# Linear attention, a routed mixture of experts and a gated layer on one core: two routing batches of four tiles, and three last tiles by one-hot matmuls

## The chip, the cores and the metric

The kernel runs on one core of a Trainium2 chip. Its engines work beside each other and meet through semaphores: TensorE (PE in the profile; PEld is its weight load), VectorE (DVE), ScalarE (ACT), GpSimd (POOL) and SyncE (SP), which issues most DMAs. The metric is the device time of one execution in microseconds; a kernel is judged by the median of several executions.

## What is computed

Three layers follow each other; everything is float32.

```python
# linear attention with decay, B, H, S, D = 2, 8, 768, 48
for t in range(S):
    cur = einsum('bhd,bhe->bhde', u * k[t], v[t])
    y[t] = einsum('bhd,bhde->bhe', r[t], state + cur)
    state = w * state + einsum('bhd,bhe->bhde', k[t], v[t])
# top-1 mixture of 8 experts over N = 1536 tokens of 384 values
expert = argmax(x @ w_gate); gate = softmax(x @ w_gate)[expert]
# token i takes the next free place of its expert (dropped past the capacity)
out[i] = gate[i] * (relu(x[i] @ w1[expert]) @ w2[expert])
# gated layer
g = x @ moe2_w_gate
return (silu(g) * (x @ moe2_w_val)) @ moe2_w_out
```

## The kernel before

The 1536 tokens are 12 tiles of 128 (NT). `attention` is a pipeline over the iterations `it`, from -4 to 12, written out by hand: the order of the calls in its loop is the order of the instructions on each engine. In iteration `it` PE makes the outputs of tile `it` (`outputs`), the token-major form and logits of tile `it` (`token_major`, into PSUM tile xl), and the inner products of tile `it + 2` (`inner`, into A). DVE multiplies in the decays of tile `it + 3` (RK), sums its diagonal factor c, and copies the masked inner products (COPY_PREDICATED). ACT builds the diagonals AT from c, and copies the outputs out of PSUM (xT, line 324; xl waits for it) and the token-major rows (xu, line 520).

Routing runs beside this in batches of tiles, listed in BATCHES. A batch whose last tile is `it - 1` is routed in iteration `it`: `route1` on DVE (lines 531 to 538) ends in the one-hot `oh` of the chosen experts, `place_pe` counts places on PE (pos, line 551), `route2` on DVE (lines 558 to 583) turns pos into the gate value m and the row in the DRAM table x_disp. Then each tile of the batch is scaled by its gate value on ACT (`scale`, line 591) and scattered into x_disp by an indirect DMA of POOL (`issue`, line 597). Tiles wait in a list `to_scatter`: an iteration scales one at its start and scatters it later, and certain iterations take extra ones out of turn.

Expert 0 would have to wait for the last tiles to arrive in x_disp. So the last NLAST tiles go into its input also by matmul: route2 makes for each a 128 x 224 one-hot `hot` (line 577, with a second `rows` call, line 571, ahead of it), and `first_add` (line 349) multiplies the tile's rows by it, three matmuls, summed in PSUM. The earlier tiles come by a DMA: `x_load` reads expert 0's first 224 rows from x_disp into xr0 (SP, line 675), issued as soon as the last tile that is not in this group has been scattered; `first_rows` (line 357) adds them to the same sum. The tiles of the group are scattered too, since another expert may need them, and those scatters wait until xr0 has been read. The last LATE tiles are routed one by one at the front of their iterations. Before, the group is tiles 8 to 11. In iteration 12 PE runs first_add of tile 10, first_add of tile 8, pos of tile 11, first_rows and first_add of tile 11; then the experts begin (line 822).

Of the kernel before, what the change touches and what calls it, by code (L numbers as in the profile page):

```python
# [11 lines left out]
F32 = mybir.dt.float32  # L12
# [11 lines left out]
P = 128  # L24
B, H, S, D = 2, 8, 768, 48
NCH = S // P
NT = B * NCH
HP = H // 2
DM = H * D
# [24 lines left out]
UC = KD * 256  # L54


NLAST, LATE = 4, 3

BATCHES = [(0, 3), (3, 6), (6, 8), (8, 9), (9, 10), (10, 11), (11, 12)]
NBT = 3  # L60
FF_WEIGHTS = {"w_gate": [P, KD, 256], "w_val": [P, KD, 256], "w_out": [P, 2, DM]}

W_LO, W_HI = 0.6, 1.6
# [6 lines left out]
class Kernel:  # L70
# [47 lines left out]
    def attention(self, st):  # L118
        tc, nc, a = self.tc, self.nc, self.a
        tp = self.tp = self.pool(st, "tp")  # L120
# [116 lines left out]
        xTs = self.xTs = {}  # L237
        self.xl, self.xu, self.batches, self.to_scatter, self.scaled = {}, {}, BATCHES, [], []
        self.row = cp.tile([P, NT], I32, name="row")

        def decay(i):
            RK[i] = tp.tile([P, 2, HP, P], F32, name="RK", tag="RK", bufs=4)

            for h in (slice(0, 2), slice(2, HP)) if i == 0 else (slice(0, HP),):
                decays[i] = nc.vector.tensor_mul(RK[i][:, :, h], rkT[i % NB][:, :, h], W2[:, :, h])
# [18 lines left out]
        def diag_act(i):  # L264
            AT[i] = tp.tile([P, 2, HP, P], F32, name="AT", tag="AT", bufs=3)
            c = cc.pop(i)
            for j in range(2):
                for hp in range(HP):
                    nc.scalar.activation(AT[i][:, j, hp], ident, AF.Copy, scale=c[:, j, hp:hp + 1])  # L269
# [35 lines left out]
        def outputs(i):  # L305

            for hp in range(HP):
                for j in range(2):
                    rows = slice(64 * j, 64 * j + D)
                    z = self.zero[rows, 0:D] if i % NCH == 0 else Z[i % 2][rows, hp]  # L310
                    nc.tensor.matmul(
                        y[rows, hp], lhsT=z, rhs=RK[i][rows, 0, hp],
                        start=(hp == 0), stop=False, skip_group_check=True,
                    )
            for hp in range(HP):
                for j in range(2):
                    nc.tensor.matmul(
                        y[64 * j:64 * j + D, hp], lhsT=head(v_all, i, 2 * hp + j), rhs=AT[i][:, j, hp],
                        start=False, stop=True, skip_group_check=True,
                    )  # L320

        def d_major(i):
            xT = xTs[i] = tp.tile([P, HP, P], F32, name="xT", tag="xT", bufs=2)
            nc.scalar.copy(xT, y)
            del RK[i], AT[i]
# [18 lines left out]
        def first_add(i, first, last):  # L344
            xu, _, hot = self.last[i]
            if first:
                px.extend(self.pa_tile() for _ in range(KD))
            for k in range(KD):
                nc.tensor.matmul(
                    px[k][:, 0:BLK], lhsT=xu[:, k * P:(k + 1) * P], rhs=hot, start=first, stop=last,  # L350
                    skip_group_check=True,
                )

        def first_rows(first):
            for k in range(KD):
                for t in range(2):
                    nc.tensor.matmul(
                        px[k][:, t * BP:(t + 1) * BP], lhsT=self.xr0[:, t, k * P:(k + 1) * P],
                        rhs=ident[0:BP, 0:BP], start=first, stop=first, skip_group_check=True,
                    )  # L360

        ok = lambda i: 0 <= i < NT
        has_state = lambda i: ok(i) and i % NCH < NCH - 1
        ends = {hi - 1: (lo, hi) for lo, hi in BATCHES}

        def issue():

            i = self.scaled[0][0]
            self.issue()
            if i == NT - NLAST - 1:  # L370
                self.x_load(0, self.xr0)
# [8 lines left out]
        for it in range(-4, NT + 1):  # L380

            if self.to_scatter:
                self.scale()
                if it >= NT - 3:
                    issue()
            batch = ends.get(it - 1)
            late = it - 1 >= NT - LATE
            if ok(it - 1):
                self.logits(it - 1)
            if ok(it):  # L390
                outputs(it)
                if not late:
                    d_major(it)
            if it == 0:
                diag_act(2)
            if batch:
                self.route1(*batch)
            if late:
                if ok(it):
                    d_major(it)  # L400
                if it - 2 >= NT - LATE:
                    first_add(it - 2, it - 2 == NT - LATE, False)
                if it == NT:
                    for i in range(NT - NLAST, NT - LATE):
                        first_add(i, False, False)
                self.place_pe(*batch)
                self.route2(*batch)
                if it == NT:
                    first_rows(False)
                    first_add(NT - 1, False, True)  # L410
            if has_state(it + 1):
                state_update(it + 1)
            if ok(it + 3):
                decay(it + 3)
                load_T(it + 3 + NB)
            if it < 0 and ok(it + 2):
                inner(it + 2)
            if ok(it + 3):
                diag_dve(it + 3)

                if it != -1:
                    diag_act(it + 3)
            if it < 0 and ok(it + 4):
                diag_pool(it + 4)
            if has_state(it + 1) and (it + 1) % NCH:
                op = state_decay(it + 1)
                if ok(it + 3):
                    behind(op, decays[it + 3])
            if it >= 0 and ok(it + 4):
                behind(diag_pool(it + 4), decays[it + 3])  # L430
            if ok(it + 4):
                keys_pool(it + 4)
                load_rk(it + 4 + NB)
            if it >= 0 and ok(it + 2):
                inner(it + 2)
            if batch and not late:
                self.place_pe(*batch)
            if self.scaled:
                issue()

            if it == NT - 5 or it == NT - 3:
                self.scale()
                issue()
            if batch and not late:
                self.route2(*batch)
            if it == -1:
                self.route_inputs(wg, cap_i)
            if it in (-1, 2, 4):
                load_v({-1: 3, 2: 6, 4: 9}[it])
            if it in (-2, 0):  # L450
                first = (it + 2) // 2 * ST
                self.clear_rows(self.x_disp[first:first + BLK])
            if ok(it):
                self.token_major(it)
            if has_state(it + 2):
                state_pe(it + 2)
            self.prefetch(it)
            if it in WARMS:
                warm(WARMS[it])
# [11 lines left out]
    def psum_rooms(self, u=False):  # L471

        bank = self.ps_1.tile([P, 512], F32, name="bank")
        n = NBT * E
        self.lgs = [bank[:, i * n:(i + 1) * n].rearrange("p (t e) -> p t e", e=E) for i in range(2)]
        self.rev = bank[:, 2 * n:2 * n + E]
        self.rank = bank[:, 2 * n + E:2 * n + E + NBT]
        self.sum = bank[:, 2 * n + E + NBT:2 * n + E + 2 * NBT]
        return bank[:, 512 - DM:] if u else None

    def route_rooms(self):
# [4 lines left out]

        self.ex = tp.tile([P, NBT, E + 1], F32, name="ex")

# [25 lines left out]
    def logits(self, i):  # L514
        nc, tp, xl = self.nc, self.tp, self.xl.pop(i)
        t = i - max(lo for lo, _ in self.batches if lo <= i)
        self.lg = self.lgs[sum(lo <= i for lo, _ in self.batches) % 2]
        nc.vector.tensor_reduce(self.lg[:, t], xl[:, :, 2 * D:].rearrange("p h e -> p e h"), AX.X, ALU.add)
        xu = self.xu[i] = self.last[i][0] if i in self.last else tp.tile([P, DM], F32, name="xu", tag="xu", bufs=6)
        nc.scalar.copy(xu.rearrange("p (h d) -> p h d", h=HP), xl[:, :, 0:2 * D])  # L520

    def route1(self, lo, hi):
# [3 lines left out]
        over_tiles = lambda x: x.unsqueeze(1).to_broadcast([P, n, E])  # L526
        small = lambda name: tp.tile([P, NBT, E], F32, name=name, tag=name, bufs=1)[:, 0:n]
        lg, oh = self.lg[:, 0:n], self.oh[:, lo:hi]
        m = self.m = tp.tile([P, 5, NBT], F32, name="m", tag="m", bufs=4)[:, :, 0:n]
        dif, eqr = small("dif"), small("eqr")  # L530
# [702 lines left out]
```

## Time and profile before

| What | us |
|---|---|
| Median of 3 runs | 453.38 (453.3 to 454.85) |
| The profiled execution | 451.36 |
| Its span, from the first to the last instruction | 449.6 |
| PE busy in the span | 432.4 (96%) |
| DVE, ACT, POOL busy | 295.1, 212.4, 156.1 |
| First matmul of the experts starts at | 79.19 |

The page of the profile gives busy time of each engine; the busy table by stage cuts the span into stretches; a timeline lists the instructions in order of time, and in brackets how long the engine stood idle before one and what ended that. A row such as `59.32 0.92 PE L512` is an instruction of line 512 that started at 59.32 us and took 0.92 us, merged with its neighbours of the same kind where it ends with x6. A float32 matmul leaves two records, so three matmuls show as x6.

### The profile page before, as it was taken

What the parts mean: (1) busy time and instruction counts of PE and PEld (TensorE: products, weight loads), DVE (VectorE), ACT (ScalarE), POOL (GpSimd) and SP (SyncE); (2) the same over time, 40 slices, a digit from 0 to 9 for tenths busy, and PEclk for the clock granted to TensorE, in tenths of its full rate; (3) what the DMA queues carried; (4) which work ended last, traced back from release to release, by engine and by line L of the source; (5) the groups of instructions that cost most, each with busy time, mean ns of one, the idle gap of its engine ahead of it and who ended that gap; (6) DMA issues with size and microseconds to landing.
All of it is one profiled execution on the core that took longest, in us unless ns stands there. A gap on an engine that the chain in (4) does not pass through costs nothing. (4 is left out here: it accounts for less than half of the span.)

```text
span 449.6 us, 8438 instructions
## 1 busy us (share of the span) xinstructions
PE 432.4 (96%) x3211; PEld 418.3 (93%) x3211; DVE 295.1 (66%) x578; ACT 212.4 (47%) x469; POOL 156.1 (35%) x147
## 2 busy tenths in 40 slices
PE   7899999999999999999999999999999999999991
PEld 7788878989999999999998999999999999999991
DVE  7989986887877977986557888979865111111110
ACT  1687774636756756755555534343343031230310
POOL 5745652201121220000343555555546233332321
PEclk9899999999999999999999999999999999999996
DMA  7998942599999999602022423242300100001001
GB/s 255 315 357 281 398 165 85 161 362 261 330 219 266 203 293 275 231 1 72 1 70 71 137 85 125 77 140 81 131 2 0 53 1 19 36 0 54 2 20 40
DMA packets 24802, 63.78 MB, mean 142 GB/s; under 512 B 4784, under 2 KB 10032, under 8 KB 24752
## 3 DMA queue, kind: packets, MB, share of 16 engines
q1 hardware_dynamic: 22112, 57.43, 40.5%
q0 software_dynamic: 1920, 4.73, 2.9%
q10 hardware_dynamic: 720, 1.00, 0.8%
q8 instruction: 27, 0.44, 0.4%
q14 instruction: 23, 0.19, 0.1%
HBM read 55.67 MB, written 7.48 MB: 140 GB/s over the span
## 5 line engine op out<-in xcount | busy, mean ns | idle before, releaser
L1034 POOL TENSOR_TENSOR al<-sg,ah 128x384 fp32r<-128x384 f32 x48 | 54.1, 1128 | 132.9 <-ACT ah L1033 132.9
L667 DVE TENSOR_TENSOR wlo<-raw,whi 128x768 fp32r<-128x768 f32 x60 | 57.2, 954 | 9.4 <-ACT whi L666 8.5
L799 PE MATMUL py<-hc,whi 128*128 128x448 f32 x192 | 63.1, 370 | 0.0
L1033 ACT CAST ah<-sg 128x384 fp32r<-128x384 f32 x48 | 24.7, 514 | 78.0 <-DVE sg L1030 78.0
L810 PE MATMUL A<-xc,whi 128*128 128x224 f32 x336 | 57.7, 276 | 1.0 <-DVE xc L683 0.9
L800 PE MATMUL py<-hc,wlo 128*128 128x256 f32 x192 | 53.8, 280 | 0.0
L810 PEld LDWEIGHTS A<-xc,whi 128*128 128x128 f32 x336 | 51.2, 192 | 1.9 <-DVE xc L683 1.5
L666 ACT CAST whi<-raw 128x768 fp32r<-128x768 f32 x60 | 49.9, 838 | 0.7 <-PE py L799 0.7
L1047 PE MATMUL po<-w_out_hi,ah 128*128 128x384 f32 x144 | 48.6, 337 | 0.0
L1049 PE MATMUL po<-w_out_hi,al 128*128 128x384 f32 x144 | 48.5, 337 | 0.0
L1048 PE MATMUL po<-w_out_lo,ah 128*128 128x384 f32 x144 | 48.5, 337 | 0.0
L810 PE MATMUL A<-xc,wlo 128*128 128x224 f32 x168 | 46.2, 275 | 0.0
L877 POOL DMA_INDIRECT ids<-tok,by_expert x12 | 13.9, 1162 | 75.0 <-DMA ids<-tok,by_expert 66.6
L1056 DVE TENSOR_TENSOR acc<-acc,po 128x384 f32<-128x384 f32 x36 | 19.3, 546 | 30.9 <-PE po L1049 30.9
L799 PEld LDWEIGHTS py<-hc,whi 128*128 128x128 f32 x192 | 36.0, 188 | 2.6
L1030 DVE TENSOR_TENSOR sg<-A,sg 128x384 f32<-128x384 f32 x24 | 13.3, 555 | 37.0 <-PE A L1027 29.3
L800 PEld LDWEIGHTS py<-hc,wlo 128*128 128x128 f32 x192 | 36.5, 190 | 0.0
L1030 DVE TENSOR_TENSOR sg<-g,sg 128x384 f32<-128x384 f32 x24 | 13.3, 555 | 34.5 <-PE g L1027 27.6
L269 ACT ACTIVATE AT<-ident,c 128x128 f32<-128x128 f32 x96 | 29.3, 389 | 9.1 <-DVE c L260 9.0
L829 ACT ACTIVATE hc<-A 128x224 fp32r<-128x224 f32 x64 | 23.1, 362 | 21.3 <-PE A L810 18.6
L810 PEld LDWEIGHTS A<-xc,wlo 128*128 128x128 f32 x168 | 32.2, 192 | 0.0
L1029 ACT ACTIVATE sg<-A 128x384 f32<-128x384 f32 x24 | 11.6, 484 | 33.8 <-PE A L1027 33.8
(171 smaller groups left out, 1106.3 us busy)
## 6 DMA issues: line engine op xcount, KB each, us to landing
raw<-in_w SPq DMA_DIRECT2D x62, 384.0 KB, 6.8
rkT<-in_rkT SPq DMA_DIRECT2D x12, 512.0 KB, 5.4
rk<-in_rk SPq DMA_DIRECT2D x12, 384.0 KB, 6.4
raw<-in_w_gate SPq DMA_DIRECT2D x6, 768.0 KB, 4.2
raw<-in_w_val SPq DMA_DIRECT2D x6, 768.0 KB, 4.2
raw<-in_w_out SPq DMA_DIRECT2D x6, 768.0 KB, 4.3
x_disp<-zero SPq DMA_DIRECT2D x8, 336.0 KB, 7.1
xr<-x_disp SPq DMA_DIRECT2D x8, 336.0 KB, 6.1
```

What stands on the lines that cost most here:

```text
L269: nc.scalar.activation(AT[i][:, j, hp], ident, AF.Copy, scale=c[:, j, hp:hp + 1])
L666: nc.scalar.copy(h_, raw)
L667: nc.vector.tensor_sub(l_, raw, h_.bitcast(F32))
L799: nc.tensor.matmul(ps[:, 0:2 * BLK], lhsT=wh, rhs=xc, start=first, stop=False, skip_group_check=True)
L800: nc.tensor.matmul(ps[:, 0:256], lhsT=wl, rhs=xc[:, 0:256], start=False, stop=last, skip_group_check=True)
L810: self.nc.tensor.matmul(ph[:, HI], lhsT=w[:, k, fs], rhs=x[1][:, k, half], start=(k == 0 and i == 0), stop=(k == KD - 1 and i == 2),)
L1030: nc.vector.tensor_mul(sg, pg["w_val"], sg)
L1033: nc.scalar.copy(h_, sg)
L1034: nc.gpsimd.tensor_sub(l_, sg, h_.bitcast(F32))
L1047: nc.tensor.matmul(po, lhsT=ah[:, ts_], rhs=wh, start=(i == 0), stop=False)
L1048: nc.tensor.matmul(po, lhsT=ah[:, ts_], rhs=wl, start=False, stop=False)
L1049: nc.tensor.matmul(po, lhsT=al[:, ts_], rhs=wh, start=False, stop=(i == len(parts) - 1))
```

## The change

Two batches of four tiles take the place of (0, 3), (3, 6) and (6, 8); the pools that hold a batch grow from three tiles to four, and the tile pool xu from six buffers to eight. NLAST falls from 4 to 3, so tile 8 has no one-hot and no first_add, and x_load follows the scatter of tile 8 instead of that of tile 7. Iteration 9 (NT - 3) takes three tiles out of turn instead of one; iteration 7 (NT - 5) still takes one.

```diff
-NLAST, LATE = 4, 3
-
-BATCHES = [(0, 3), (3, 6), (6, 8), (8, 9), (9, 10), (10, 11), (11, 12)]
-NBT = 3
+NLAST, LATE = 3, 3
+
+BATCHES = [(0, 4), (4, 8), (8, 9), (9, 10), (10, 11), (11, 12)]
+NBT = 4
...
-            if it == NT - 5 or it == NT - 3:
+            for _ in range({NT - 5: 1, NT - 3: 3}.get(it, 0)):
                 self.scale()
                 issue()
...
-        xu = self.xu[i] = self.last[i][0] if i in self.last else tp.tile([P, DM], F32, name="xu", tag="xu", bufs=6)
+        xu = self.xu[i] = self.last[i][0] if i in self.last else tp.tile([P, DM], F32, name="xu", tag="xu", bufs=8)
```

On ACT in iterations 7 to 9 there stood before (xu written by L591 is a scaling in place, by L520 the copy of a tile's rows; xu_209 is tile 8's copy, xs_210 its scaled rows):

```order
L591 ACTIVATE xu<-xu,m 128x384 x2
L520 COPY xu<-xl 128x384
L324 COPY xT<-y 128x512
L533 ACTIVATE ex<-dif 128x2x8
L269 ACTIVATE AT<-ident,c 128x128 x8
L591 ACTIVATE xu<-xu,m 128x384
L520 COPY xu_209<-xl 128x384
L324 COPY xT<-y 128x512
L533 ACTIVATE ex<-dif 128x8
L591 ACTIVATE xu<-xu,m 128x384
L591 ACTIVATE xs_210<-xu_209,m 128x384
```

And now, from the same scaling of iteration 7:

```order
L591 ACTIVATE xu<-xu,m 128x384
L520 COPY xu<-xl 128x384
L324 COPY xT<-y 128x512
L533 ACTIVATE ex<-dif 128x4x8
L269 ACTIVATE AT<-ident,c 128x128 x8
L591 ACTIVATE xu<-xu,m 128x384
L520 COPY xu<-xl 128x384
L324 COPY xT<-y 128x512
L533 ACTIVATE ex<-dif 128x8
L591 ACTIVATE xu<-xu,m 128x384 x4
```

The pair ahead of xT of tile 8 (the first L324 of each list) has become one scaling; after the exp of tile 8, four scalings (tiles 5 to 8) stand where there were two (tiles 7 and 8).

On POOL, the scatters (L597) from iteration 7 on, before (L378 is the decay of the state, xs_210 to xs_219 are tiles 8 to 11):

```order
L597 DMA x_disp<-xu,row 14080x384 x2
L378 TENSOR_TENSOR Z_134<-zt,sq 112x192
L597 DMA x_disp<-xu,row 14080x384 x2
L378 TENSOR_TENSOR Z_135<-zt,sq 112x192
L597 DMA x_disp<-xu,row 14080x384
L597 DMA x_disp<-xs_210,row 14080x384
L597 DMA x_disp<-xs_213,row 14080x384
L597 DMA x_disp<-xs_216,row 14080x384
L597 DMA x_disp<-xs_219,row 14080x384
```

And now (xs_210 to xs_216 are tiles 9 to 11):

```order
L597 DMA x_disp<-xu,row 14080x384 x2
L378 TENSOR_TENSOR Z_134<-zt,sq 112x192
L597 DMA x_disp<-xu,row 14080x384
L378 TENSOR_TENSOR Z_135<-zt,sq 112x192
L597 DMA x_disp<-xu,row 14080x384 x4
L597 DMA x_disp<-xs_210,row 14080x384
L597 DMA x_disp<-xs_213,row 14080x384
L597 DMA x_disp<-xs_216,row 14080x384
```

Behind the last decay stand four scatters (tiles 5 to 8) ahead of the load of xr0, where one (tile 7) stood; tile 8's was behind the load.

On PE from xl of tile 11 to the count, before (hot_211 belongs to tile 8, hot_217 to tile 10, hot_220 to tile 11):

```order
L512 MATMUL xl<-IW,xT 128x104 x4
L349 MATMUL A<-hot_217,xu_215 128x224 x3
L349 MATMUL A<-hot_211,xu_209 128x224 x3
L551 LDWEIGHTS before
L551 MATMUL pos<-oh,before 128x8
L551 LDWEIGHTS ones_bf
L551 MATMUL pos<-ohs,ones_bf 128x8
L357 MATMUL A<-ident,xr 128x112 x6
L349 MATMUL A<-hot_220,xu_218 128x224 x3
```

And now (hot_214 belongs to tile 10, hot_217 to tile 11):

```order
L512 MATMUL xl<-IW,xT 128x104 x4
L349 MATMUL A<-hot_214,xu_212 128x224 x3
L551 LDWEIGHTS before
L551 MATMUL pos<-oh,before 128x8
L551 LDWEIGHTS ones_bf
L551 MATMUL pos<-ohs,ones_bf 128x8
L357 MATMUL A<-ident,xr 128x112 x6
L349 MATMUL A<-hot_217,xu_215 128x224 x3
```

The three matmuls of tile 8 between those of tile 10 and pos of tile 11 are gone.

## Rows read from the trace of the kernel before

**Rows 1.** Busy by stage: stretch, length, PE, PEld, DVE, ACT, POOL, clock, DMA share, GB/s.

```profile
36.00:60.00 24.00, 23.60 (x357) 20.26 (x356) 22.64 (x60) 19.94 (x59) 15.36 (x17) 1.00 0.89 329
79.20:97.00 17.80, 17.75 (x105) 17.11 (x103) 15.25 (x39) 8.72 (x17) 2.78 (x3) 1.00 0.74 239
```

**Rows 2.** Timeline, 57 to 60 us: start, duration, engine, line, operation [idle before].

```profile
57.32 1.11 ACT L591 ACTIVATE xu<-xu,m 128x384 f32<-128x384 f32 x2
...
58.20 1.33 POOL L597 DMA_INDIRECT x_disp<-xu,row  x1 [1.53 <-ACT xu L591]
...
58.69 0.58 ACT L324 COPY xT<-y 128x512 f32<-128x512 f32 x1
...
59.32 0.92 PE L512 MATMUL xl<-IW,xT 128*128 128x104 f32 x6 [0.37 <-ACT xT L324]
```

**Rows 3.** Timeline, 64 to 68.5 us (end of iteration 9, iteration 10).

```profile
64.17 1.34 DVE L283 COPY_PREDICATED AT<-mask,A 128x512 f32<-128x512 uint8 x2 [0.73 <-PE A L276]
64.68 1.01 POOL L597 DMA_INDIRECT x_disp<-xu,row  x1 [0.17 <-issue]
...
66.17 0.15 DVE L571 SCALAR_TENSOR_TENSOR m<-bank,placeall 128x1 f32<-128x1 f32 x1
66.35 0.62 ACT L591 ACTIVATE xs<-xu,m 128x384 f32<-128x384 f32 x1 [2.08 <-DVE m L571]
...
66.67 0.15 DVE L571 SCALAR_TENSOR_TENSOR row<-bank,placeall 128x1 int32<-128x1 f32 x1
...
66.94 0.19 DVE L518 TENSOR_REDUCE bank<-xl 128x8 f32<-128x32 f32 x1
...
67.16 0.48 ACT L520 COPY xu<-xl 128x384 f32<-128x384 f32 x1 [0.19 <-DVE bank L518]
...
67.43 0.33 SPq L675 DMA_DIRECT2D xr<-x_disp  x1
...
67.74 0.57 ACT L324 COPY xT<-y 128x512 f32<-128x512 f32 x1
...
68.18 0.17 PE L551 MATMUL pos<-oh,before 128*128 128x8 bf16 x1 [0.98 <-DVE oh L538]
...
68.36 0.36 PE L512 MATMUL xl<-IW,xT 128*128 128x104 f32 x1
```

**Rows 4.** Timeline of PE, 74 to 80 us (iteration 12).

```profile
74.08 2.54 PE L349 MATMUL A<-hot,xu 128*128 128x224 f32 x12 [0.23 <-DVE hot L577]
76.46 0.17 PE L551 MATMUL pos<-oh,before 128*128 128x8 bf16 x1
...
76.51 1.57 PE L357 MATMUL A<-ident,xr 112*128 112x112 f32 x12
77.95 1.37 PE L349 MATMUL A<-hot,xu 128*128 128x224 f32 x6
```

**Rows 5.** Timeline of DVE, 75 to 79.5 us (routing of tile 11).

```profile
75.25 0.16 DVE L538 TENSOR_TENSOR oh<-eqr,bank 128x8 bf16<-128x8 f32 x1
...
76.69 0.17 DVE L562 SCALAR_TENSOR_TENSOR sc<-pos,oh 128x8 f32<-128x8 f32 x1 [0.99 <-PE pos L551]
...
77.41 0.40 DVE L577 TENSOR_SCALAR hot<-slot,m 128x224 f32<-128x224 f32 x1
```

**Rows 6.** Timeline of POOL, 57 to 80 us: scatters of tiles 8 and 9.

```profile
71.23 0.96 POOL L597 DMA_INDIRECT x_disp<-xs,row  x1 [5.54 <-DVE bank L559]
72.49 0.96 POOL L597 DMA_INDIRECT x_disp<-xs,row  x1 [0.30 <-ACT xT L324]
```

**Rows 7.** DMA issues, 66 to 70 us, then the whole span: KB, us to landing.

```profile
xr<-x_disp SPq DMA_DIRECT2D x1, 336.0 KB, 3.0
xr<-x_disp SPq DMA_DIRECT2D x8, 336.0 KB, 6.1
```

**Rows 8.** Busy table by stage around the early fall of the granted clock.

```profile
14.40:15.80 1.40, 0.06 (x3) 0.09 (x5) 1.37 (x4) 0.43 (x2) 1.34 (x2) 1.00 0.92 309
15.80:19.30 3.50, 3.50 (x42) 3.01 (x44) 3.03 (x5) 2.02 (x7) 3.50 (x3) 0.51 0.87 300
```

## The prediction

> **What bounds the kernel now.** I read the busy table by stage first. From 79.2 us on, TensorE (PE) is busy almost without a break (17.75 of 17.80 us in the next stage), and nothing there is touched, so whatever moves the start of the first expert (the 79.2 us mark) moves the end by as much. From 36 to 60 us PE is busy 23.60 of 24.00 us while VectorE (DVE) has 22.64 [rows 1]: PE is the bound of the steady loop, and DVE work taken away there is worth only what PE waits for. So I looked next, on the timelines, for each place where PE waits in the iterations that change, and for what ends that wait. There are three.
>
> At 59.32 us PE waits 0.37 us for the ScalarE (ACT) copy xT of tile 8. That copy stands behind two scalings in a row (1.11 us from 57.32) and begins at 58.69 [rows 2]. At 68.18 PE waits 0.98 us for the one-hot `oh` of tile 9, made on DVE. DVE had started the copies of iteration 9 at 64.17 (after PE), then ran route2 of tile 8 until 66.94, then the logits and route1 of tile 9; behind it ACT makes scaling, xu and xT, and xT of tile 10 (67.74 + 0.57) releases xl at 68.36 [rows 3]. From 74.08 on PE runs 12 matmul records of first_add without a wait, six of tile 10 and six of tile 8, then pos, first_rows and first_add of tile 11 [rows 4].
>
> **The change part by part.** *Batches.* Seven batches become six. The batch that goes (tiles 3 to 5) is 12 small DVE instructions like those of [rows 3], 0.15 to 0.19 us each, about 2 us in iteration 6; but PE bounds that stage, so by itself this is worth nothing; of the small pos matmuls 18 become 17. What counts is where the scalings land: ACT no longer has two in a row ahead of xT of tile 8 (its list shows one, since the four tiles of the first batch are scaled over iterations 5 to 7 and the second batch is not routed yet). One scaling less is about half of 1.11 us, more than the 0.37 us that PE waits. **Term 1: 0.37 us.** Bounds: 0, if c, which DVE hands to ACT, comes later, and 0.55, half of the pair.
>
> *Tile 8 leaves the one-hot group (NLAST 4 to 3).* On DVE, route2 of tile 8 loses the second `rows` and `hot`: from 66.17 to 66.67, 0.50 us, between PE's inner of iteration 9 and the logits of tile 9 [rows 3]. So the logits of tile 9 come 0.37 + 0.50 = 0.87 us earlier, at 66.07, and `oh` lets PE go at 67.31. PE's own outputs move by 0.37 only, so the wait there falls to about 0.48 us. But xl of tile 10 wants xT, and ACT is next in line: the scaling of tile 8 starts after m, now 66.17 - 0.37 = 65.80, plus 0.03 and 0.62 is 66.45; its successor overlaps by some 0.05, so xu starts at 66.40 rather than 67.16, and xT and xl move by 0.76, not 0.87. **Terms 1 and 2 together: 0.76 us** at xl of tile 10 (68.36 to 67.60); bounds 0.39 (term 1 at nothing) and 1.05 (term 1 at 0.55, ACT not in the way).
>
> On PE the six records of first_add of tile 8 go. Twelve take 74.08 to 76.46, so six take 1.19 us [rows 4]. They were cover: `oh` of tile 11 is written at 75.25 to 75.41 [rows 5], and 0.76 us earlier is 74.65. PE is done with tile 10 at 74.08 - 0.76 + 1.19 = 74.51 and then waits for it until about 74.70. pos of tile 11 thus moves from 76.46 to 74.70. Behind it first_rows (76.51 to 77.95, 1.44 us) hides `hot` of tile 11: DVE took 1.12 us from sc at 76.69 to the end of hot at 77.81 [rows 5], so hot is ready at 74.93 + 1.12 = 76.05, and PE comes to first_add of tile 11 at 74.75 + 1.44 = 76.19. **Term 3: 1.00 us** (1.19 less 0.19 of uncovered wait); bounds 0.9 and 1.19.
>
> *The scatters and the load xr0.* This is what could spoil it. The load of expert 0's rows now follows tile 8's scatter instead of tile 7's, and the second batch's four scalings all fall into iteration 9. On ACT three scalings of about 0.55 us sit after exp of tile 8; before the change ACT stood idle 2.08 us ahead of tile 8's scaling [rows 3], which covers the two that are new there. On GpSimd (POOL) one scatter, a decay and four scatters now stand in a row. Before, the scatter behind the decay began at 64.68 [rows 3], now 0.37 earlier, 64.31. Three more steps of 1.18 us (1.01 + 0.17 of issue, the spacing of rows behind other work), or 1.26 us as 71.23 to 72.49 shows [rows 6], put tile 8's scatter at 67.85 to 68.09; I take 1.26, a real pair of scatters. Its scaling is done at 66.45, so POOL sets the time. SyncE (SP) began the load at 67.43 after a scatter begun at 64.68, 2.75 us; the load landed in 3.0 us [rows 3, 7]. That gives 68.09 + 2.75 + 3.0 = 73.84. first_rows wants it at 74.75, so 0.9 us of slack hides it. If each scatter took the longest seen, 1.33 us [rows 2], with 0.17 of issue, the load lands at 74.56, still in time. Scatters 9 to 11 must wait until this load has been read, as tile 8's did at 71.23 [rows 6]; tile 11's own scaling is later than that, so they delay nothing. Nothing but expert 1's load waits behind xr0 on SP, and that waits for the last scatter anyway. **Term 4: 0.**
>
> *Sizes.* The wider pool of xu and the wider batch tiles change addresses; the batch instructions grow from 24 to 32 columns on an engine with room in that stage [rows 1]: nothing.
>
> Sum: 0.76 + 1.00 = **1.76 us**. The profiled execution, 451.36 us with a span of 449.6, would become 449.6 with a span of 447.8. The median of the runs is 453.38, so it lies 2.0 us above the profiled one; I take the gain off the median: **451.6 us**, which is 0.39% less. A measurement of this kernel tells about 0.5%, 2.27 us, from no change, so the forecast lies inside "same", on the fast side. By the terms' bounds the gain is 1.3 to 2.2 us, 451.2 to 452.1.
>
> **The rivals.** *A little more (451.0 us).* Term 1 is 0.55, ACT does not hold xT of tile 10, `oh` of tile 11 is no wait: 1.05 + 1.19 is 2.24, and some 0.1 from smaller waits that DVE's lead removes in iterations 4 to 7. For it: DVE has two microseconds less to do. Against: PE had next to no idle time there to give back [rows 1].
>
> *The scatters stretch (452.4 us).* If the load lands about 0.8 us after first_rows wants it, half of the gain is gone. For it: five scatters now lie on one queue. Against: the scatter at 64.68 ran through a DVE copy (64.17, 1.34 us) and took 1.01 us [rows 3], no longer than others. The Trainium skill, SBUF — State Buffer, section "Who interferes with whom", says that descriptor generation on GpSimd is locked out while certain copies, casts and tensor_scalar instructions of VectorE hold the shared port. By that rule the copy beside a scatter would add its 1.34 us to the row, and the load would land at 75.2, some 0.4 us late; the scatter beside the copy here shows no such stretch, so I give it little.
>
> *Slower (455.5 us).* The load lands as late as the median of its eight kind, 6.1 us instead of 3.0 [rows 7]: 76.94 instead of 73.84. First_rows then starts 0.4 us later than before, and PE has stood idle for 2.2 us. That has a price of its own: after 1.40 us with 0.06 us of PE work the granted clock was 0.51 for 3.5 us, the 1.2 GHz level [rows 8], which costs 3.5 x 0.49 = 1.7 us. Together 2.1 us above the median. It decides from a landing of about 5.7 us. Against: the 6.1 belongs to loads beside the weight stream; here the weight loads are over and the one measured in this place took 3.0. The Trainium skill, TensorE: Matmul & The Clock Gate, section "HAM oscillation — how this bites in real kernels", says that gaps between matmuls caused by waiting for a load throttle the clock again; this trace agrees at 15.8 us, and shows no drop after the 0.98 us gap at 68.18.
>
> *It doesn't do what it says.* If xT of tile 8 is late for another reason and ACT holds xl, only the six records count: 1.0 to 1.4 us, 452.0 to 452.4.
>
> **How the numbers follow.** Forecast 0.58; a little more 0.15; stretched or only the matmuls 0.19; slower 0.08. The runs before scatter from 453.3 to 454.85 with the profiled one at 451.36, so a gain of 1.76 can be measured above 2.27; I move 0.08 of the forecast there: faster 0.23, same 0.69, slower 0.08. The range takes in 451.0 with the runs' scatter below it, and the stretched case with some scatter above: 450.4 to 453.4; the slow rival is left out.
>
> **What would show it.** Right: on PE no wait before xl of tile 8; the wait for `oh` of tile 9 near 0.5 us; pos of tile 11 right after three first_add matmuls (six records); the first matmul of expert 0 at about 77.4 instead of 79.19; the load of xr0 landed a microsecond ahead of first_rows. Wrong: PE waiting for a DMA ahead of first_rows, a granted clock under 1 after 60 us, scatters spaced by far more than 1.3 us, or xl of tile 8 still waiting for xT.

## The result, and the profile after

The changed kernel takes **457.88 us** (456.17 to 459.24, six runs) where the kernel before takes 453.19 (six runs): a ratio of 1.0091, 95% interval 1.0064 to 1.0119. It is slower; 451.6 was forecast and 453.4 was the top of the range. The profiled execution took 456.97 us with a span of 455.2, so the span grew by 5.6 us.

The timeline of TensorE (PE) in the changed kernel, to be held against [rows 3] and [rows 4]:

```profile
62.96 1.12 PE L512 MATMUL xl<-IW,xT 128*128 128x104 f32 x8
64.00 1.08 PE L311 MATMUL y<-RK,Z 48*48 48x128 f32 x16
65.01 1.08 PE L317 MATMUL y<-AT,v_all 128*48 128x128 f32 x16
66.58 0.17 PE L551 MATMUL pos<-oh,before 128*128 128x8 bf16 x1 [0.49 <-DVE bank L537]
66.61 0.17 PE L551 MATMUL pos<-ohs,ones_bf 128*128 128x8 bf16 x1
70.39 2.04 PE L512 MATMUL xl<-IW,xT 128*128 128x104 f32 x8 [3.62 <-ACT xT L324]
72.36 1.95 PE L311 MATMUL y<-RK,Z 48*48 48x128 f32 x16
...
80.38 1.57 PE L357 MATMUL A<-ident,xr 112*128 112x112 f32 x12
...
83.05 2.14 PE L822 MATMUL A<-x_plain,raw 128*128 128x224 f32 x10
```

Up to pos of tile 9 everything is as forecast: the wait for `oh` is 0.49 us (0.98 before), and pos stands at 66.58 where it stood at 68.18. Then PE stands still for 3.62 us before xl of tile 10, which before started 0.18 us behind pos. What it waits for is the ScalarE (ACT) copy xT, and that copy and VectorE's (DVE) next step were themselves kept waiting. The timelines of ACT and DVE:

```profile
69.76 0.59 ACT L324 COPY xT<-y 128x512 f32<-128x512 f32 x1 [3.41 <-remote]
```

```profile
69.80 0.17 DVE L562 SCALAR_TENSOR_TENSOR sc<-pos,oh 128x8 f32<-128x8 f32 x1 [2.99 <-remote]
```

Both are free, and both want only a semaphore that PE raises. The copy needs the outputs of tile 10, whose last matmul ended at 65.01 + 1.08 = 66.09; `sc` needs pos, done by 66.78. Both start within 0.04 us of each other, at 69.76 and 69.80: 3.67 and 3.02 us after PE was through. "remote" is the profile's word where it finds no instruction that ended just then. In the trace's semaphore events the two increments of PE stand at 69.73 and 69.78. By the profile PE's work was done, and nobody was told. (The ends of matmuls are modelled times; that PE had gone past the outputs is also seen from pos, which started behind them at 66.58.)

The busy table of chosen stretches shows what the standstill cost beyond itself. Columns: stretch, busy time of PE, PEld, DVE, ACT and GpSimd (POOL), then the granted clock.

```profile
15.80:19.30 3.50, 3.29 (x57) 2.68 (x51) 3.14 (x6) 2.28 (x7) 3.50 (x3) 1.00 0.93 275
66.10:69.70 3.60, 0.19 (x2) 0.11 (x2) 0.61 (x5) 0.25 (x2) 2.13 (x3) 1.00 0.42 153
69.70:76.50 6.80, 6.11 (x41) 5.15 (x42) 2.55 (x15) 2.14 (x5) 0.96 (x1) 0.50 0.28 90
76.50:103.80 27.30, 26.10 (x156) 24.27 (x156) 21.43 (x65) 13.35 (x27) 4.31 (x4) 1.00 0.60 194
103.80:107.30 3.50, 3.50 (x19) 3.50 (x18) 2.31 (x5) 1.68 (x4) 0.58 (x1) 0.51 1.03 392
```

After 3.6 us with 0.19 us of PE work the granted clock is 0.50 for 6.8 us, the 1.2 GHz level: the matmuls of tile 11's outputs take 1.95 us where the same ones of tile 10 took 1.08. A second fall, 0.51 for 3.5 us, comes at 103.8.

The 5.6 us, by marks: pos of tile 9 is 1.60 early; xl of tile 10 is 2.03 late (70.39 against 68.36), so the standstill costs 3.63; the first matmul of expert 0 starts at 83.05, 3.86 late (79.19 before), so the stretch between lost another 1.83, put down to the half clock less the matmuls that went; the second fall costs 3.5 x 0.49 = 1.7, together 5.6.

What does POOL do during the standstill? Its timeline:

```profile
62.31 1.01 POOL L597 DMA_INDIRECT x_disp<-xu,row  x1 [2.94 <-DVE eqr L534]
63.35 0.52 POOL L378 TENSOR_TENSOR Z<-zt,sq 112x192 f32<-112x192 f32 x1
64.03 1.01 POOL L597 DMA_INDIRECT x_disp<-xu,row  x1 [0.17 <-ACT xu L591]
65.35 0.96 POOL L597 DMA_INDIRECT x_disp<-xu,row  x1 [0.30 <-issue]
66.61 0.96 POOL L597 DMA_INDIRECT x_disp<-xu,row  x1 [0.30 <-ACT ex L533]
67.88 0.96 POOL L597 DMA_INDIRECT x_disp<-xu,row  x1 [0.31 <-issue]
```

The row of scatters is there as forecast, 1.26 us apart, tile 8's at 67.88 (68.09 forecast). Before, the last scatter ahead of this place began at 64.68 [rows 3]. xT starts 1.88 us after the last scatter began.

### The profile page after: what moved, and what is told of

Read it like the earlier page. It is cut to its first block, busy times and chain, and to the rows that moved or that the text cites. A ratio compares the mean times of both kernels' runs of the same rounds, so it can differ in the third digit from the quotient of the medians.

```text
span 455.2 us, 8403 instructions
## 1 busy us (share of the span) xinstructions
PE 433.9 (95%) x3204; PEld 419.5 (92%) x3204; DVE 293.4 (64%) x564; ACT 212.8 (47%) x468; POOL 155.4 (34%) x147
## 5 line engine op out<-in xcount | busy, mean ns | idle before, releaser
L810 PE MATMUL A<-xc,whi 128*128 128x224 f32 x336 | 59.2, 280 | 1.0 <-DVE xc L683 0.8
L810 PEld LDWEIGHTS A<-xc,whi 128*128 128x128 f32 x336 | 52.6, 196 | 1.9 <-DVE xc L683 1.4
```

Source lines behind the costliest of these rows:

```text
L810: self.nc.tensor.matmul(ph[:, HI], lhsT=w[:, k, fs], rhs=x[1][:, k, half], start=(k == 0 and i == 0), stop=(k == KD - 1 and i == 2),)
```

## The experiments

"Late" is, from the timelines of ACT and PE, the start of the copy xT of tile 10 less the end of the last matmul of outputs of tile 10. "After last scatter" is the start of that copy less the start of the last scatter before it. In before, e4 and e13 what is late is ACT itself, which still ran the exp ahead of the copy; PE's increment came at once. The runs took five chips: one had e1 to e4, the others e5 to e8, e9 to e12, e13 to e15, and e16 with e17.

| Kernel | us, median | Ratio to before, 95% | Late, us | After last scatter, us |
|---|---|---|---|---|
| before | 453.19 | | 0.54 | 3.06 |
| after | 457.88 | 1.0091 (1.0064 to 1.0119) | 3.67 | 1.88 |
| e1 after +64 | 450.97 | 0.9966 (0.9932 to 0.9999) | 0.15 | 0.08 |
| e2 after -16 | 451.86 | 0.9952 (0.9917 to 0.9988) | 0.15 | 0.07 |
| e3 after +8 | 450.11 | 0.9935 (0.9906 to 0.9965) | 0.15 | 0.08 |
| e4 before +8 | 452.36 | 0.9980 (0.9954 to 1.0007) | 0.55 | 3.07 |
| e5 after, again | 457.17 | 1.0051 (0.9976 to 1.0127) | 3.32 | 1.98 |
| e6 after +4 | 457.52 | 1.0072 (1.0023 to 1.0121) | 3.34 | 2.00 |
| e7 after -8 | 457.78 | 1.0071 (1.0025 to 1.0117) | 3.34 | 2.00 |
| e8 after, 16 between | 457.65 | 1.0083 (1.0033 to 1.0133) | 3.35 | 2.00 |
| e9 after, again | 457.63 | 1.0091 (1.0070 to 1.0111) | 3.25 | 1.89 |
| e10 after +8 | 457.13 | 1.0081 (1.0046 to 1.0117) | 3.25 | 1.92 |
| e11 after +4 | 457.72 | 1.0087 (1.0061 to 1.0113) | 3.24 | 1.89 |
| e12 after +64 | 456.33 | 1.0058 (1.0019 to 1.0097) | 3.25 | 1.90 |
| e13 before, 3 x tile 7 | 456.13 | 1.0036 (0.9999 to 1.0073) | 0.80 | 3.31 |
| e14 after, tile 8 moved | 458.56 | two runs, no interval | 1.85 | 1.78 |
| e15 after, tiles 7, 8 moved | 450.76 | 0.9951 (0.9913 to 0.9990) | 0.40 | 1.59 |
| e16 before, held back | 456.08 | 1.0074 (1.0038 to 1.0109) | 2.37 | 1.79 |
| e17 as e15 | 451.29 | 0.9949 (0.9923 to 0.9975) | 0.47 | 1.66 |

### First theory: a load of TensorE's instructions (e1 to e4)

Beside the standstill the trace of the changed kernel shows a 16 KB load of PE's own instructions (67.51 to 68.73 us), and the increments came a microsecond after it had ended. The first theory was that PE's stream ran onto the end of a loaded section just where all else waited. It was tested by moving everything in PE's stream by a few instructions: tiny matmuls behind the first warm-up, or the same warm-up columns in fewer matmuls.

```diff
-        def warm(n):
+        def warm(n, tiny=0):
             junk = self.pa_tile()
             for _ in range(n):
                 nc.tensor.matmul(junk[:, 0:P], lhsT=ones, rhs=ones, start=True, stop=True)
-
-        warm(WARM)
+            for _ in range(tiny):
+                nc.tensor.matmul(junk[0:1, 0:1], lhsT=ones[:, 0:1], rhs=ones[:, 0:1], start=True, stop=True)
+
+        warm(WARM, 2)
```

That is e3 and e4 (two matmuls, each 4 of PE's instructions); e6 has one, e1 and e12 have 16. e2 and e7 write the 11 warm-up matmuls with four and two of double width.

> The changed kernel with 16 one-column matmuls more (64 TensorE instructions) behind the first warm-up, so that everything behind them stands 64 places later in TensorE's instruction stream; the work is otherwise the same. Theory (instruction load): in the changed kernel the two semaphore increments of outputs of tile 10 and pos of tile 9 came 3.6 and 3.0 us late because a 16 KB load of TensorE's instructions (67.51 to 68.73 us) fell where the engine had nothing but waiting work; 64 places are about 3.5 us of TensorE work, so the load moves to about 63 to 64.5 us, under the dense outputs of tile 10, the increments come within 0.1 us, xl of tile 10 starts near 67.4 instead of 70.39, no clock fall at 69.7, span 447.5 to 450, ratio to the kernel before 0.993 to 1.000. Rival (five scatters in a row hold the increments up): stall and clock fall stay, span 454 to 457, ratio near 1.009.

> The changed kernel with 11 warm-up matmuls of 128 columns written as 3 of 128 and 4 of 256: same columns, 16 TensorE instructions fewer. Theory (instruction load): the load starts 16 places later in the work, when xl of tile 10 is already running and dense work follows, so no late increments: xl of tile 10 near 67.4, span 447.5 to 450, ratio 0.993 to 1.000. If the load begins while TensorE still stands before xl, the stall is shorter but there, span 450 to 455. Rival (scatters): stall of about 3 us and clock fall stay, ratio near 1.009.

> The changed kernel with 2 one-column matmuls more (8 TensorE instructions). Theory (instruction load): the load moves by only 8 places, about 0.4 us, into the last matmuls of the outputs of tile 10; the increments of outputs(10) and pos(9) are still caught, 2.5 to 3.6 us late, xl of tile 10 at 69.5 to 70.4, span 453 to 457, ratio 1.004 to 1.010. Rival (scatters): the same stall, ratio near 1.009; this run alone does not tell them apart, it shows how near the boundary has to be.

> The kernel before with 2 one-column matmuls more (8 TensorE instructions) behind the first warm-up. Theory (instruction load): there the load began at 69.95 us, behind xl of tile 10; 8 places earlier its start falls between the end of outputs(10) and pos(9), where TensorE waits 0.98 us for the one-hot: the increments of outputs(10) come 2 to 3 us late, xl of tile 10 starts at 70 to 71 instead of 68.36, the clock falls behind it, span 452 to 456, ratio 1.004 to 1.012. If 8 places are too few to reach it: ratio 1.000 within 0.002. Rival (scatters in a row): the scatters are those of before, nothing changes, ratio 1.000.

All three shifted kernels lost the standstill, and the theory looked confirmed, though e3, whose 8 places were expected to be too few, lost it as well. e4 did not get it.

### The control that took the theory down (e5 to e12)

> The changed kernel unchanged, once more. Theory (instruction load at this exact place of the stream): the stall comes back in this profile, increments of outputs(10) and pos(9) 3 to 3.6 us late beside the load of TensorE's instructions, clock fall behind it, time 456 to 459. Rival (a chance of the first runs or of their chip): the increments come at once, xl of tile 10 near 67, time 449.5 to 452 like the shifted kernels.

> The changed kernel with one one-column matmul more (4 TensorE instructions), half of the shift that already took the stall away. Theory (exact place): if the place has to be met within 4, no stall, 449.5 to 452; if it is as wide as 4 to 8, stall, 455 to 459. Rival (chance): no stall in this nor in the unshifted kernel.

> The changed kernel with 8 TensorE instructions fewer (11 warm-up matmuls written as 7 of 128 columns and 2 of 256). Theory (exact place): the 16 fewer of the second run had no stall, 8 fewer lie nearer: no stall if the place is narrow (449.5 to 452), a stall of up to 3 us if the load now begins while TensorE stands before xl of tile 10 (453 to 459). Rival (chance): no stall here nor in the unshifted kernel.

```diff
+        for _ in range(8 if lo == 9 else 0):
+            nc.tensor.matmul(
+                pos[0:1, 3, 0:1], lhsT=self.ones_bf[:, 0:1], rhs=self.ones_bf[:, 0:1], start=True, stop=True,
+                skip_group_check=True
+            )
```

> The changed kernel with 8 one-element bfloat16 matmuls (16 TensorE instructions) between pos and xl of tile 10 alone, into unused columns of pos: everything up to pos(9) keeps its place in the stream, and only what stands behind moves by 16. Theory A (it counts where the waiting xl of tile 10 stands in the stream): no stall, xl of tile 10 near 67.3, 449.5 to 452. Theory B (it counts where outputs(10) and pos(9), whose increments were late, stand): the stall stays, 455 to 459. Rival (chance): no stall here nor in the unshifted kernel.

All four stood still, at four places in the stream. That fits a window of places, but also the chip, since these four ran on another one. So the shifted kernels were run again beside the unshifted one:

> The changed kernel unchanged, on one chip with the shifted ones. The four kernels without the stall (+64, -16, +8 and the kernel before +8) ran on one chip, the four with it (0, +4, -8 and 16 between) on another, so place in the stream and chip are not told apart yet. Theory P (place in TensorE's instruction stream): stall here, increments of outputs(10) over 3 us late, 456 to 459. Theory C (chip): this goes as the other three of this call, whichever way.

> The changed kernel with 8 TensorE instructions more, on the same chip as the unchanged one. Theory P (place): no stall, 449 to 452. Theory C (chip): as the unchanged one beside it.

> The changed kernel with 4 TensorE instructions more, on the same chip as the unchanged one. Theory P (place): stall, 456 to 459. Theory C (chip): as the unchanged one beside it.

> The changed kernel with 64 TensorE instructions more, on the same chip as the unchanged one. Theory P (place): no stall, 449 to 453. Theory C (chip): as the unchanged one beside it.

All four stood still. e3 and e10 are one kernel on two chips. PE in e3, then in e10:

```profile
66.65 0.17 PE L551 MATMUL pos<-oh,before 128*128 128x8 bf16 x1 [0.49 <-DVE oh L538]
...
66.94 1.14 PE L512 MATMUL xl<-IW,xT 128*128 128x104 f32 x8
```

```profile
66.84 0.17 PE L551 MATMUL pos<-oh,before 128*128 128x8 bf16 x1 [0.70 <-DVE bank L537]
...
70.02 2.04 PE L512 MATMUL xl<-IW,xT 128*128 128x104 f32 x8 [3.00 <-ACT xT L324]
```

The place in PE's stream is not the cause. The load of instructions isn't either: in e6 it began at 66.68 and in e7 at 74.36, before and behind the standstill, and both increments came 3.3 us late all the same. What stays constant is the last column of the table: on one chip the copy starts 1.98 to 2.00 us after the last scatter of the row began, on another 1.89 to 1.92. And wherever else such a trace shows late increments of PE, a scatter began shortly before. In e10, for instance, the increment for U is 0.45 us late at 50.43, beside a scatter at 50.30, and DVE's zt, which waits for it, starts 0.54 us after the end of U where it starts 0.15 after it in e3; PE had work there and lost nothing. DVE in e3, then in e10:

```profile
50.60 0.36 DVE L303 TENSOR_TENSOR zt<-U,Z 112x192 f32<-112x192 f32 x1 [0.26 <-PE U L291]
```

```profile
50.97 0.36 DVE L303 TENSOR_TENSOR zt<-U,Z 112x192 f32<-112x192 f32 x1 [0.67 <-PE U L291]
```

On the chip of e1 to e4 no increment of PE in the whole trace of e3 was more than 0.05 us late, beside the same row of scatters.

### Second theory: the row of scatters (e13 to e17)

The theory: while POOL issues one scatter after the other, PE's increments are held up until the row is through. The rival: it is something else that the change moved. e14 and e15 take one and two scatters out of the row by scaling these tiles behind the copy xT of tile 10 (e15 shown; in e14 the 2 is 1 and the 3 stays):

```diff
-            if self.to_scatter:
+            if self.to_scatter and it != NT - 2:
                 self.scale()
...
                 if ok(it):
                     d_major(it)
+                for _ in range(2 if it == NT - 2 else 0):
+                    self.scale()
+                    issue()
...
-            for _ in range({NT - 5: 1, NT - 3: 3}.get(it, 0)):
+            for _ in range({NT - 5: 1, NT - 3: 2}.get(it, 0)):
```

> The changed kernel, tile 8's scaling and scatter moved behind the copy xT of tile 10, so that the row is four scatters (the last at 66.2 instead of 67.5) and tile 8's comes after the wait. Theory S: the hold ends with the fourth scatter, the increments of outputs(10) and pos(9) come 1.3 to 2 us late instead of 3.2, xl of tile 10 near 68 to 69 instead of 70; span 450 to 454. Rival: the increments are as late as before, about 3.2 us, ratio near 1.009.

Here the last scatter of the row began at 73.62 and xT 1.78 later. The profiled execution ran some 7 us late from before this place, so only distances within the place are used, and its time not at all. PE waited 1.61 us, against 2.78 to 3.62 with the whole row:

```profile
76.04 2.04 PE L512 MATMUL xl<-IW,xT 128*128 128x104 f32 x8 [1.61 <-ACT xT L322]
```

> The changed kernel, scalings and scatters of tiles 7 and 8 moved behind the copy xT of tile 10: a row of three scatters that ends at about 65.9 us, ahead of the end of outputs(10). Theory S: increments of outputs(10) and pos(9) 0 to 0.8 us late, xl of tile 10 at 66.9 to 67.7, no clock fall there; xr0 lands at about 74.5, on the edge of what first_rows wants; ratio 0.992 to 0.999. Rival: stall of about 3.2 us stays, ratio near 1.009.

POOL, ACT and PE of e15 (the line numbers up to 360 have moved by two or three):

```profile
65.46 0.96 POOL L597 DMA_INDIRECT x_disp<-xu,row  x1 [0.30 <-issue]
68.43 0.96 POOL L597 DMA_INDIRECT x_disp<-xu,row  x1 [2.01 <-DVE m L571]
69.69 0.96 POOL L597 DMA_INDIRECT x_disp<-xu,row  x1 [0.30 <-issue]
```

```profile
67.05 0.59 ACT L322 COPY xT<-y 128x512 f32<-128x512 f32 x1
...
71.37 0.59 ACT L322 COPY xT<-y 128x512 f32<-128x512 f32 x1 [1.56 <-PE y L315]
```

```profile
67.36 0.17 PE L551 MATMUL pos<-oh,before 128*128 128x8 bf16 x1 [0.71 <-DVE oh L538]
...
67.69 1.14 PE L512 MATMUL xl<-IW,xT 128*128 128x104 f32 x8
...
75.24 1.59 PE L354 MATMUL A<-ident,xr 112*128 112x112 f32 x12 [0.24 <-DMA xr<-x_disp]
```

The row ends with the scatter at 65.46, the increment is 0.4 us late, xl has no wait, and the price of moving two scatters is 0.24 us at xr0. This chip does hold: e14 shows it, and here the moved pair (68.43 and 69.69) makes the copy xT of tile 11 start 0.52 us after its outputs ended at 70.85, where e1 has 0.05; PE had work there. The kernel is 0.49% faster than before. e17 repeats it on a fifth chip:

> The changed kernel with the scalings and scatters of tiles 7 and 8 behind the copy xT of tile 10, once more. Theory S: increments of outputs(10) and pos(9) at most 0.8 us late on any chip, no clock fall behind them, ratio 0.992 to 0.999. If the earlier result was that chip's alone: stall of 2 to 3 us, ratio 1.005 to 1.010.

0.47 us late, ratio 0.9949; PE waited 0.19 us before xl and 0.40 for xr0. This version beats the kernel before on two chips that hold. The changed kernel itself was not run on these two; it takes 457.2 to 457.9 on the others that hold.

The other direction is to give the kernel before a row. e13 issued tile 7's scatter three times:

> The kernel before with the scatter of tile 7 issued three times in a row instead of once (same rows to the same places), so that GpSimd scatters at about 64.7, 65.9 and 67.2 us, across the end of outputs(10) at 67.2; nothing else is changed. Theory S (a scatter holds TensorE's increments up until it is through): outputs(10)'s increment comes only at 68.6 to 69.2 instead of 67.2, xl of tile 10 at 69.2 to 70 instead of 68.36, the clock may fall, ratio 1.002 to 1.010. Rival (something else of the change, or a hold that needs the changed tiles): the increments come at once; xr0 lands 2.5 us later, still ahead of first_rows or less than a microsecond behind it, ratio 0.998 to 1.003. On a chip without late increments at any other scatter the run tells nothing.

It tested nothing: each copy waited for the one ahead to land, so they began at 67.21, 70.58 and 75.10 and no row stood across the outputs. What it lost is the load of xr0, 1.39 us late for first_rows. e16 makes the row out of scatters that are there anyway:

```diff
-            if self.to_scatter:
+            if self.to_scatter and it != NT - 4:
                 self.scale()
...
-            if it == NT - 5 or it == NT - 3:
+            for _ in range(3 if it == NT - 3 else 0):
                 self.scale()
                 issue()
```

> The kernel before, batches and one-hots unchanged; iterations 7 and 8 each hold back one scaling and scatter, so that iteration 9 takes three out of turn and GpSimd scatters tiles 5, 6 and 7 in a row at about 64.7, 65.9 and 67.2 us, across the end of outputs(10) at 67.2. Theory S (the row holds TensorE's increments up): the increments of outputs(10) and pos(9) come 1 to 2.5 us late, xl of tile 10 at 69 to 71 instead of 68.36, the clock falls to 0.5 for some us behind it, span 451.5 to 456, ratio 1.003 to 1.011. Rival (it needs the changed batches or one-hots): increments at once, ratio 0.998 to 1.002. On a chip without late increments at any other scatter the run tells nothing.

POOL and PE of e16, then the granted clock (last but two) behind it:

```profile
66.52 1.01 POOL L597 DMA_INDIRECT x_disp<-xu,row  x1 [0.17 <-ACT xu L591]
67.83 1.01 POOL L597 DMA_INDIRECT x_disp<-xu,row  x1 [0.30 <-issue]
69.15 0.96 POOL L597 DMA_INDIRECT x_disp<-xu,row  x1 [0.30 <-ACT xu L520]
```

```profile
67.49 1.08 PE L317 MATMUL y<-AT,v_all 128*48 128x128 f32 x16
69.43 0.17 PE L551 MATMUL pos<-oh,before 128*128 128x8 bf16 x1 [0.86 <-DVE oh L538]
...
71.58 1.14 PE L512 MATMUL xl<-IW,xT 128*128 128x104 f32 x8 [1.96 <-ACT xT L324]
```

```profile
70.00:77.00 7.00, 5.42 (x44) 4.71 (x45) 2.55 (x15) 2.46 (x5) 0.65 (x2) 0.76 0.24 80
```

With the batches, one-hots and matmuls of before, the row alone makes xT 2.37 us late (PE's increment stands at 70.92, so this is not ACT's own work), stops PE for 1.96, drops the clock and costs 0.74%. The scalings moved together with the scatters in e14 to e17; what tells the two apart is time, since the three moved scalings of e16 had ended by 66.99. So the row is the cause on the chips that hold, and the new batches matter only because they made it.

## Why the prediction was wrong

**Terms 1 to 3 held.** e1 to e3 are the change without the hold. By marks, PE in e1, then in before:

```profile
54.44 1.14 PE L512 MATMUL xl<-IW,xT 128*128 128x104 f32 x8
...
59.26 1.12 PE L512 MATMUL xl<-IW,xT 128*128 128x104 f32 x8
...
63.98 1.12 PE L512 MATMUL xl<-IW,xT 128*128 128x104 f32 x8
...
67.89 1.14 PE L512 MATMUL xl<-IW,xT 128*128 128x104 f32 x8
...
77.72 7.62 PE L822 MATMUL A<-x_plain,raw 128*128 128x224 f32 x39
```

```profile
54.05 1.14 PE L512 MATMUL xl<-IW,xT 128*128 128x104 f32 x8
...
64.06 1.12 PE L512 MATMUL xl<-IW,xT 128*128 128x104 f32 x8
```

From xl of tile 7 to tile 8 e1 takes 4.82 us (before 5.27): 0.45, where 0.37 was forecast. The wait is gone, and xl now starts at 59.26, ahead of the end of the last pos matmul, from which the profile had counted the wait. From xl of tile 9 to tile 10, 3.91 (before 4.30): 0.39, as forecast, so terms 1 and 2 give 0.84 for 0.76. From xl of tile 10 to the first expert, 9.83 (before 10.83): 1.00 for 1.00. The sum is 1.84 for 1.76; e2 and e3 agree with e1, and e4 with before, within 0.02 at each of these marks. The medians of e1 to e3 lie 1.5 to 3.3 us below their kernel before, and the forecast of 0.39% lies in all three intervals; e4, which does no less work than before, lies 1.0 below it too, so the medians tell the size less well than the marks. On that chip the forecast was right in step and size.

**Term 4 failed.** It put the row of scatters at nothing, on the argument that only the load of xr0 waits for it, and priced it by when the data lands. The times of the row were right (67.88 for tile 8, the load issued at 70.49 for 70.84), and first_rows found xr0 there (80.38, no wait, though by then it was late itself; in e1, without the hold, the load was issued at 71.04, landed in 2.9 us, and first_rows came 1.1 us later without a wait). What was missing is that a row of scatters can cost engines that want nothing from it: the rows of before showed single scatters and one pair, where PE had other work, and I read "POOL is off the path" from them. They could not have shown more: in the trace of before no increment of PE is more than 0.05 us late beside any scatter, as on the chip of e1 to e4. The term should have had a bound from the other side: what if PE's next increment came only after the row. By the row's end, 67.88 + 1.9 against 66.1, that is the 3.6 us that came.

**The rivals.** "Scatters stretch" looked at the length of a scatter: those of the row took 0.96 to 1.01 us each, no stretch. (One scatter outside the row was longer, 1.43 us at 57.40 and 2.05 at 57.35 in e1.) The lock-out of GpSimd that the Trainium skill, SBUF — State Buffer, section "Who interferes with whom", states does not show in the row, and that section tells of no delay of semaphores. "Slower" had the right sign and the right second half, idle PE and then a half clock, with the wrong cause and half of the size: it idled 2.2 us and fell for 3.5, where PE idled 3.6 and the clock fell for 6.8. The Trainium skill, TensorE: Matmul & The Clock Gate, section "HAM oscillation — how this bites in real kernels", has PE throttled again in gaps in which its matmuls wait for a load. The gap here had another cause; the trace agrees with 0.50 after 3.6 us. The list of signs did name the granted clock under 1 after 60 us.

**The clock.** Two more falls differ between executions and were not foreseen. Before had one at 15.8 us [rows 8], the profiled changed kernel none there (1.00 in the table of stretches). Some 0.6 of its 1.60 us lead at pos of tile 9 was there by xl of tile 7 and is put down to this, which no run isolates (from xl of tile 7 to pos of tile 9 e1 takes 13.16 us and before 14.13, 0.97 less). The fall at 103.8 follows two waits, 0.16 and 0.68 us, that before has too (0.18 and 0.67) without one; what decides it is open.

## What to carry to other kernels

A queue off the critical path is not free because nobody waits for its results: before packing indirect DMAs into a row, look what runs beside it, and keep rows away from places where the main engine has nothing queued but work that hangs on its own last result. Where a wait is put down to nothing the profile knows ("remote"), look at when the producer's work ended and at what another engine was doing until the wait ended. And repeat a surprising control on the same chip before believing a shift: three changed kernels looked "fixed" here only by where they ran. A trace from one chip can lack a cost that another chip has.

## What the runs showed of the hardware

On four of the five chips of the experiments, and on the one of the result, TensorE's semaphore increments came late beside GpSimd's scatters: 0.3 to 1.1 us beside single ones, and in a row until 1.6 to 2.0 us after the last had begun, each lasting 0.96 to 1.01 us. By the DMA packets of the traces, the data of a row's last scatter began to move some 1.54 us after it (at 75.16 in e14, 70.68 in e16), and the held increments followed 0.03 to 0.43 us behind (75.38, 70.92), before the data had landed. On the fifth chip none was late beside the same row. DVE's one-hot released PE during the row without such a delay (pos of tile 9 at 66.58, while `oh` ended at 66.53), so the hold is shown for PE's increments only. Some semaphore records are missing from the traces, most of them from those of the holding chips, so single late records count for less than the waits behind them. What holds the increments, and why one chip does not, stays open. Whether other DMAs of POOL do the same was not tried; beside its gathers in the experts' stage no increment of PE that can be told is more than 0.3 us late.
